# One pool of five PSUM banks, held-back stores, and part of the q norms off TensorE

## The chip, the cores and the metric

The kernel runs on one core of a Trainium2 chip. Its time is the device time in microseconds (us) of one execution; a kernel's figure is the median of several runs. The profile is of one execution of its own, and its times are counted from the start of its span.

The engines are named TensorE (PE in the profile, its weight loads PEld), VectorE (DVE), ScalarE (ACT), GpSimd (POOL) and SyncE (SP). Each runs its instructions in the order in which the program lists them, and waits on semaphores for the others.

## The reference

```python
def _attn_ref(q, k, v, tau):            # B, N, C = 4, 6336, 256
    qn = q / (np.linalg.norm(q, axis=1, keepdims=True) + 1e-06)
    kn = k / (np.linalg.norm(k, axis=1, keepdims=True) + 1e-06)
    s = kn.transpose(0, 2, 1) @ qn / tau
    s = s - s.max(-1, keepdims=True)
    a = np.exp(s)
    a /= a.sum(-1, keepdims=True) + 1e-09
    return (v @ a).astype(np.float32)

def _moe_ref(x, w_h, w_t, b_t):         # x: 25344 x 256, the rows of all batches
    H = np.maximum(x @ w_h, 0.0)
    T = 1.0 / (1.0 + np.exp(-(x @ w_t + b_t)))
    return (T * H + (1.0 - T) * x).astype(np.float32)
```

For each of four batches, q and k (6336 rows of 256 channels, f32) give one 256 x 256 attention matrix over channels: products over the rows, divided by the norms of the columns, and a softmax. Each row of v is then multiplied by that matrix, and the result x goes through a highway layer: two more products, a relu, a sigmoid and a mix.

## The kernel before, in words

**Stage 1.** A batch's rows are taken in 50 steps: 48 of 128 rows, in six chunks of eight steps, and two tail steps of 96 rows. A load of one chunk of q, k or v reads 1 MB of f32 and writes 0.5 MB of f16; it is issued by GpSimd (`load`, L286 and L281). For each step and each half c of the channels, `stage1` makes three matmuls into the PSUM tile `sg[c]`: k by q (256 columns, L393), k by k (128 columns, L394) and q by q (128 columns, L395). The diagonals of the last two are the squared norms of the columns of k and q.

**The chain.** After a batch's last step `plan_chain` makes a softmax out of `sg`: diagonals (VectorE), square roots (GpSimd, `pow`, L452), reciprocals, a broadcast over partitions (TensorE, `cqb`), exponentials (ScalarE), a transposition (`eps`) and a product with the two weight matrices (`fold`, `ah`). It ends in the f16 tile `mr`, which holds the attention matrix and its products with both weights, so that stage 2 needs v alone.

**Stage 2.** The 50 steps of v are taken in 25 pairs a batch; the pairs of all batches are numbered g = 0 to 99. For batches 0 to 2, v is transposed on TensorE (L612) and evicted by VectorE or ScalarE into `vtsb`. For the last batch (`by_dma`) SP issues one DMA transpose a chunk (`transpose_chunk`, L620) into `vT`, of which there are four buffers. Each pair then has three products of four matmuls each, all of line L642: `h`, `t` and `x` (the latter is written into the bank of `d`). ScalarE or VectorE copies the bias into t's bank ahead of t (`bias`, L405 and L407), or in the last part, on odd pairs beyond g = 65, a matmul does (L673). ScalarE makes relu(h)/2 into `d` (L682) and a tanh of t (`gate`, L696); VectorE makes the product (L703) and the result (L722). Results gather in an `o` tile of one chunk (four pairs, 1 MB), which SP stores (L736).

**PSUM.** Of eight banks, `sg0` and `sg1` hold stage 1, `vt` serves the transposes, and five are given by name: `h` two, `d` two, `t` one. After stage 1 of the last batch `sg0` also serves h and `sg1` also serves t.

**What sets the order.** The program is written by a planner. `plan.add` makes a task of one engine with a key (mostly the pair's number g plus an offset: the smallest key of those that can start goes first), a pitch, a latency, the tasks that it depends on, and the buffers that it takes and gives back. `Plan.run` plays this with the planner's own costs and lists the instructions in the order in which they start. Loads go to GpSimd in one fixed order, eight in flight at most; stores and DMA transposes go to SP, by key. On the chip every engine keeps the order so found. `slot_of` spreads the steps of stage 1 of batches 1 to 3 over the pairs: `ENDS = [18, 42, 66]` are the pairs at which the three end. Stage 1 of batch b + 1 so runs among the pairs of batch b.

## Time and profile before

| | |
|---|---|
| median of 7 runs | 279.61 us (279.0 to 280.04) |
| the profiled execution's own time | 278.93 us |
| its span | 277.2 us |
| busy in the span: PE, DVE, ACT, POOL | 254.6, 181.6, 175.1, 54.6 us |
| granted TensorE clock | 0.994 |
| bytes read from and written to HBM | 78.38 MB, 25.95 MB |
| stage 1 of batches 0 to 3 ends at | 38.7, 94.3, 155.4, 216.7 us |
| first matmul of h of pairs 0, 24, 48, 66, 75, 99 | 47.2, 111.2, 172.6, 215.8, 235.7, 269.8 us |
| matmuls of q by q (L395), steps of 128 rows | 384 |
| last load issued, last load landed | 219.8, 234.4 us |

In the profile a line such as `L395 PE MATMUL sg<-q` names the line of the kernel, the engine, the operation and the tiles (written<-read). "Releaser" is what ended an engine's idle time. A line of waits has who waited, for whom, the total in us, how often, and the longest. A line of stretches has the bounds in us, the length, then busy us (and instructions) of PE, PEld, DVE, ACT and POOL, the granted clock, the mean busy share of the 16 DMA engines (above 1 where transfers overlap on an engine) and the GB/s that they moved, counted as written. A line of the list of instructions has start and duration in us. Matmuls are pipelined: a matmul's duration is longer than the distance to the next.

### The profile page before, as it was taken

The page shows a single profiled execution, that of the slowest core. Times are in us where ns is not written, and L with a number is a line of the kernel's source. Part 1 is how long each engine was busy: PE and PEld are TensorE (multiplying, and loading weights), DVE is VectorE, ACT ScalarE, POOL GpSimd, SP SyncE. Part 2 cuts the span into 40 slices and gives each one's busy share as a digit, 9 for nine tenths or more (in the row PEclk, how much of TensorE's full clock was granted, in tenths as well). Part 3 has the DMA queues.
Part 4 walks back from the last instruction along what each step waited for, and adds up shares of the span by engine and source line. Part 5 has one row for each costly group of instructions (what it writes and reads, how often), then busy time and mean ns, then how long its engine had stood idle before and what let it go on. Part 6 is the DMA issues. An engine that isn't in the chain of part 4 may idle for free.

```text
span 277.2 us, 6499 instructions
## 1 busy us (share of the span) xinstructions
PE 254.6 (92%) x2610; PEld 227.7 (82%) x2610; DVE 181.6 (66%) x366; ACT 175.1 (63%) x328; POOL 54.6 (20%) x104
## 2 busy tenths in 40 slices
PE   0797879999999999999999999999999888999992
PEld 0596877899999888999999888999999767888881
DVE  1000035667766886777776886777777887898994
ACT  1000016667767776776767766777767779898982
POOL 7222445220212230211112421111111300000000
PEclk9997999999999999999999999999999999999999
DMA  6999999999999999999999999999999999999984
GB/s 109 212 216 212 208 208 213 215 212 286 263 248 277 285 217 283 245 268 287 237 262 288 254 245 279 222 295 263 248 280 286 233 266 176 356 205 313 269 307 180
DMA packets 29581, 68.80 MB, mean 248 GB/s; under 512 B 14832, under 2 KB 16496, under 8 KB 26608
## 3 DMA queue, kind: packets, MB, share of 16 engines
q0 software_dynamic: 12608, 39.20, 71.5%
q1 hardware_dynamic: 16944, 29.20, 31.5%
q8 instruction: 20, 0.33, 0.4%
q14 instruction: 9, 0.07, 0.1%
HBM read 78.38 MB, written 25.95 MB: 376 GB/s over the span
## 4 chain that ended last, share of the span: by engine, by line
PE 55%; DMA 39%; POOL 2%; DVE 2%; issue 1%; ACT 0%; POOLq 0%; DVEq 0%; ACTq 0%
DMA v<-in_v_dram 19%; PE h L642 11%; PE t L642 11%; PE d L642 10%; PE sg L393 9%; DMA k<-in_k_dram 7%; DMA vT<-v 7%; DMA q<-in_q_dram 7%; PE sg L394 4%; PE sg L395 4%; PE vtps L612 3%; PE t L673 1%; DVE pp L703 1%; POOL q L286 1%; PE ah L551 1%
## 5 line engine op out<-in xcount | busy, mean ns | idle before, releaser
L393 PE MATMUL sg<-q,k 128*128 128x256 f16 x384 | 95.8, 280 | 13.6 <-DMA k<-in_k_dram 13.6
L642 PEld LDWEIGHTS <-vtsb 128*128 128x128 f16 (+1 forms) x900 | 83.4, 99 | 9.8 <-issue 1.9
L394 PE MATMUL sg<-k 128*128 128x128 f16 x384 | 86.2, 225 | 0.0
L395 PE MATMUL sg<-q 128*128 128x128 f16 x384 | 85.4, 222 | 0.0
L703 DVE SCALAR_TENSOR_TENSOR pp<-uu,d 128x512 f32<-128x512 f32 (+1 forms) x100 | 68.4, 685 | 17.2 <-PE d L642 12.0
L696 ACT ACTIVATE uu<-t 128x512 f32<-128x512 f32 (+1 forms) x100 | 59.6, 598 | 27.3 <-PE t L642 25.4
L682 ACT ACTIVATE d<-h 128x512 f32<-128x512 f32 (+1 forms) x100 | 58.4, 584 | 22.3 <-PE h L642 22.0
L722 DVE SCALAR_TENSOR_TENSOR o<-h,pp 128x512 f32<-128x512 f32 x96 | 66.2, 690 | 2.9
L393 PEld LDWEIGHTS <-k 128*128 128x128 f16 x384 | 38.4, 100 | 16.3 <-DMA k<-in_k_dram 14.6
L405 ACT COPY t<-bias_all 128x512 f32<-128x512 f32 (+1 forms) x78 | 46.0, 589 | 2.0
L642 PE MATMUL d<-mr,vtsb 128*128 128x256 f16 x300 | 44.8, 272 | 0.1
L642 PE MATMUL t<-mr,vtsb 128*128 128x256 f16 x300 | 44.8, 272 | 0.1
L642 PE MATMUL h<-mr,vtsb 128*128 128x256 f16 x300 | 44.8, 272 | 0.0
L407 DVE COPY vtsb<-vtps 128x256 f32<-128x256 f32 (+1 forms) x62 | 26.1, 421 | 26.2 <-PE vtps L612 25.9
L395 PEld LDWEIGHTS <-q 128*128 128x128 f16 x384 | 38.6, 100 | 5.4
L394 PEld LDWEIGHTS <-k 128*128 128x128 f16 x384 | 38.6, 100 | 1.9
L642 PEld LDWEIGHTS <-vT 128*128 128x128 f16 x288 | 28.1, 98 | 5.7 <-DMA vT<-v 1.0
L612 PE MATMUL vtps<-ident,v 128*128 128x128 f32 x144 | 27.7, 274 | 1.8 <-ACT vtsb L405 1.1
L441 DVE SCALAR_TENSOR_TENSOR junk<-sg,ident 128x128 f32<-128x128 f32 x16 | 4.6, 287 | 37.0 <-PE sg L395 36.4
L484 ACT COPY gs<-sg 128x256 f32<-128x256 f32 x8 | 2.6, 377 | 37.8 <-DVE junk L441 37.8
L286 POOL DMA_DIRECT2D v<-in_v_dram x24 | 13.1, 544 | 47.0 <-PE d L642 15.5
L286 POOL DMA_DIRECT2D k<-in_k_dram x25 | 13.5, 539 | 42.3 <-DMA k<-in_k_dram 15.7
(66 smaller groups left out, 176.9 us busy)
## 6 DMA issues: line engine op xcount, KB each, us to landing
out_dram<-o SPq DMA_DIRECT2D x23, 1024.0 KB, 8.9
v<-in_v_dram POOLq DMA_DIRECT2D x24, 512.0 KB, 20.6
q<-in_q_dram POOLq DMA_DIRECT2D x23, 512.0 KB, 21.5
k<-in_k_dram POOLq DMA_DIRECT2D x23, 512.0 KB, 20.6
out_dram<-o SPq DMA_DIRECT2D x2, 512.0 KB, 2.6
out_dram<-ot SPq DMA_DIRECT2D x4, 192.0 KB, 6.7
q<-in_q_dram POOLq DMA_DIRECT2D x2, 256.0 KB, 14.5
k<-in_k_dram POOLq DMA_DIRECT2D x2, 256.0 KB, 11.1
```

What stands on the lines that cost most here:

```text
L286: nc.gpsimd.dma_start(out=t[:, s : s + n, :], in_=main_rows(src)[:, j * CH + s : j * CH + s + n, :])
L393: nc.tensor.matmul(sg[c][:, 0:C], kc, qa, start=first, stop=False)
L394: nc.tensor.matmul(sg[c][:, C : C + P], kc, kc, start=False, stop=False)
L395: nc.tensor.matmul(sg[c][:, C + P : C + 2 * P], qa[:, cs], qa[:, cs], start=False, stop=last)
L405: nc.scalar.copy(out=out, in_=in_)
L407: nc.vector.tensor_copy(out=out, in_=in_)
L612: nc.tensor.transpose(ps[:, u, 0:nr], words, ident0[0:nr, 0:nr])
L642: nc.tensor.matmul(out[0:nr, u, :], vt[u][kt][:, 0:nr], mr[kt][:, col * C : (col + 1) * C], **flags(u, kt))
L682: nc.scalar.activation(out=d[0:nr, :, :], in_=ps_t["h", b, i][0:nr, :, :], func=Act.Relu, scale=0.5)
L696: nc.scalar.activation(out=uu[0:nr, :, :], in_=ps_t.pop(("t", b, i))[0:nr, :, :], func=Act.Tanh, scale=-0.5)
L703: nc.vector.scalar_tensor_tensor(out=pp[0:nr, :, :], in0=el.pop(("uu", b, i))[0:nr, :, :], scalar=1.0, in1=ps_t.pop(("d", b, i))[0:nr, :, ...
L722: nc.vector.scalar_tensor_tensor(out=ot, in0=ps_t.pop(("h", b, i))[0:nr, :, :], scalar=0.0, in1=el.pop(("pp", b, i))[0:nr, :, :], op0=AluO ...
```

## The change

- `plan_squares`, `squares`, `sum_squares`: for the first four chunks (`APART = 4`) of batches 1 to 3 the q-by-q matmuls are left out. ScalarE squares the chunk in two halves of 128 x 1024 into f32, GpSimd adds these up to 128 x 256 (three or four additions a chunk, with the one to the batch's sum), two matmuls of one column each sum over the partitions, and VectorE adds the result to the diagonals.
- `Plan.banks`: the five banks that were h, t and d are common. A task that needs one names how many must be free (`spare`: h 3, t and its bias 2, relu and chain steps 1) and takes the one free for longest. `adds` and `sets` note in which banks a matmul may accumulate onto what another engine wrote; `spread` prepares all five (before: three). In the last part `sg0`, `sg1` and `vt` join. The chain takes its banks here too.
- `plan_holds`, `hold`: up to pair 64 (`UNTIL`) the store of a chunk comes after a 1 KB copy on SP that reads the first result of the chunk five later (`LAG`); `o` has seven buffers (before: three). Later stores have keys of at least 65.6.
- Batch 3's chunk 0 of v is transposed on TensorE as f16 (`BY_DMA = 1`); the others by DMA with a key 18 pairs ahead (before: 8); `vT` has three buffers.
- Batch 0's last chunk comes after the tail, in four parts (before: ahead of the tail in the loop, in two parts), and `consts.serial` puts the constants behind the first two loads on GpSimd.
- Buffers: q and k five each (before: nine), v five (before: seven), `vtsb` nine (before: five). Keys come from a table `PRIO` with one offset up to pair 66 and one beyond; `ENDS` is 22.5, 38 and 66; the bias is put in by matmul on even pairs beyond 66; the four matmuls of a product go kt by kt.

```diff
--- before.py
+++ after.py
-QK_BUFS = 9
-V_BUFS = 7
-AHEAD = 8
-MOVE = 100e3
-LOOK = 1.6
-POW = 1.0
-HEAD = 8
-TAIL = 65
+QK_BUFS = 5
+V_BUFS = 5
+O_BUFS = 7
+LAG = 5
+UNTIL = 64
+AHEAD = 18
+BY_DMA = 1
+MOVE = 150e3
+APART = 4
+V_AHEAD = 4
+PRIO = {
+    "tr": (-3.46, 4.45), "ev": (5.77, -0.35), "h": (-3.36, 2.13), "bias": (2.76, -0.39),
+    "t": (-0.61, -1.32), "relu": (0.66, 0.05), "x": (-0.27, -1.65), "gate": (1.05, 1.05),
+    "prod": (-3.53, 1.79), "res": (0.54, -1.85), "s1": (0.08, -2.66), "sq": (3.14, 1.81),
+}
+POW = 0.75
+HEAD = 10
+TAIL = 66
+EVERY = 2
 EV = BIAS = ("ACT", "DVE")
-ENDS = [18, 42, 66]
+ENDS = [22.5, 38, 66]
...
+                and (not x.spare or bank_for(x) is not None)
...
+        def bank_for(x):
+            open_ = [(a, n) for n, (a, _) in self.banks.items() if a is not None and a <= t + eps]
+            if len(open_) < x.spare:
+                return None
+            if x.adds:
+                open_ = [(a, n) for a, n in open_ if self.banks[n][1]]
+            else:
+                open_ = [(a, n) for a, n in open_ if not self.banks[n][1]] or open_
+            return min(open_)[1] if open_ else None
...
         "q": QK_BUFS, "k": QK_BUFS, "v": V_BUFS, "tail_q": 2, "tail_k": 2, "tail_v": 2,
-        "vT": 4, "vT_t": 1, "o": 3, "ot": 1, "uu": 3, "pp": 3, "vtsb": 5, "mr0": 2, "mr1": 2,
-        "sg0": 1, "sg1": 1, "vt": 1, "t": 1, "h": 2, "d": 2,
+        "sq": 2, "vT": 3, "vT_t": 1, "o": O_BUFS, "ot": 1, "uu": 3, "pp": 3, "vtsb": 9, "mr0": 2, "mr1": 2,
+        "sg0": 1, "sg1": 1, "vt": 1,
     }
     for tag, bufs in nbuf.items():
         plan.ring(tag, bufs)
-    pool_of = {tag: psum for tag in ("sg0", "sg1", "vt", "t", "h", "d")}
+    common = [f"c{n}" for n in range(5)]
+    nbuf |= {tag: 1 for tag in common}
+    pool_of = {tag: psum for tag in ["sg0", "sg1", "vt"] + common}
...
     plan_load("q", 0, 0)
     plan_load("k", 0, 0)
     consts = plan.add("POOL", len(plan.tasks), 0.6, 1.5, [], constants)
+    consts.serial = True
     for j in range(1, NJ - 1):
         plan_load("q", 0, j)
         plan_load("k", 0, j)
     for nm in "qk":
         plan_load(nm, 0, NJ)
-    plan_load("q", 0, NJ - 1, 2)
-    plan_load("k", 0, NJ - 1, 2)
+    for part in range(4):
+        plan_load("q", 0, NJ - 1, 4, part)
+        plan_load("k", 0, NJ - 1, 4, part)
...
-                seq.append((NP * b + CH // 2 * j - (10 if b == B - 1 else 2), 1, "v", b, j))
+                seq.append((NP * b + CH // 2 * j - V_AHEAD, 1, "v", b, j))
...
-            nc.tensor.matmul(
-                sg[c][:, C + P : C + 2 * P], qa[:, cs], qa[:, cs], start=False, stop=last
-            )
+            if not apart(b, s // CH):
+                nc.tensor.matmul(
+                    sg[c][:, C + P : C + 2 * P], qa[:, cs], qa[:, cs], start=False, stop=last
+                )
...
+    def apart(b, j):
+        return b > 0 and j < APART
+    sq_t = {}
+    sums = {}
+    def squares(b, j, half):
+        sq_t[b, j, half] = sq = new("sq", [P, CH // 2, C], f32, f"sq{b}_{j}_{half}")
+        qa = tiles[("q", b, j)][:, half * CH // 2 : (half + 1) * CH // 2, :]
+        nc.scalar.activation(out=sq, in_=qa, func=Act.Square)
+    def sum_squares(b, j, step):
+        add = partial(nc.gpsimd.tensor_tensor, op=AluOp.add)
+        if step == 0:
+            sq, other = sq_t[b, j, 0], sq_t.pop((b, j, 1))
+            add(out=sq, in0=sq, in1=other)
+        elif step == 1:
+            sq = sq_t[b, j, 0]
+            add(out=sq[:, 0:2, :], in0=sq[:, 0:2, :], in1=sq[:, 2:4, :])
+        else:
+            sq = sq_t.pop((b, j, 0))
+            if j == 0:
+                sums[b] = small.tile([P, C], f32, tag="sums", name=f"sums{b}")
+                add(out=sums[b], in0=sq[:, 0, :], in1=sq[:, 1, :])
+            else:
+                add(out=sq[:, 0, :], in0=sq[:, 0, :], in1=sq[:, 1, :])
+                add(out=sums[b], in0=sums[b], in1=sq[:, 0, :])
...
+    def plan_squares(b):
+        ends, x = {}, None
+        for j in range(APART):
+            key = slot_of((b - 1) * NS + CH * j) + PRIO["sq"][0]
+            parts = [
+                plan.add(
+                    "ACT", key, 0.97, 1.07, loaded("q", b, CH * j + CH // 2 * n),
+                    lambda j=j, n=n: squares(b, j, n), take=["sq"],
+                )
+                for n in range(2)
+            ]
+            ends[j] = parts
+            n0 = len(plan.tasks)
+            y = plan.add(
+                "POOL", key, 2.36, 2.45, parts, lambda j=j: sum_squares(b, j, 0), drop=[(parts[1], "sq")]
+            )
+            y = plan.add("POOL", key, 1.27, 1.35, [y], lambda j=j: sum_squares(b, j, 1))
+            x = plan.add(
+                "POOL", key, 1.3 if j else 0.65, 1.4 if j else 0.75, [y] + ([x] if x else []),
+                lambda j=j: sum_squares(b, j, 2), drop=[(parts[0], "sq")],
+            )
+            for z in plan.tasks[n0:]:
+                z.soft = True
+        def over_partitions():
+            sums[b, "ps"] = ps = new("vt", [P, 2], f32, f"sumps{b}")
+            for c in range(2):
+                nc.tensor.matmul(
+                    ps[:, c : c + 1], sums[b][:, bass.ts(c, P)], ones[:, 0:1], start=c == 0, stop=c == 1
+                )
+        def keep():
+            sums[b, "sb"] = sb = small.tile([P, 2], f32, tag="sumsb", name=f"sumsb{b}")
+            nc.vector.tensor_copy(out=sb, in_=sums[b, "ps"])
+        p = plan.add("PE", key + 2, 0.4, 0.6, [x], over_partitions, take=["vt"])
+        return ends, plan.add("DVE", key + 1, 0.15, 0.22, [p], keep, drop=[(p, "vt")])
...
+        def rest_of_q():
+            if sums_of_q:
+                xq = st["x"][:, 0:2]
+                nc.vector.tensor_tensor(out=xq, in0=xq, in1=sums[b, "sb"], op=AluOp.add)
+        dq = dve(
+            lambda: (diagonal(0), diagonal(1), rest_of_q()), 0.9, 0.95, [last, consts] + sums_of_q
+        )
         nq = pool(lambda: norm(0), POW, POW + 0.2, [dq])
         dk = dve(lambda: (diagonal(2), diagonal(3)), 0.75, 0.8, [dq])
...
+        if b == B - 1:
+            gs.joins = [("sg0", True), ("sg1", True)]
...
-            st["cqb"] = new("vt", [P, C], f32, f"cqb{b}")
+            st["cqb"] = new(cqb.bank, [P, C], f32, f"cqb{b}")
...
-        cqb = pe(bcast, 0.43, [iq], take=["vt"])
+        cqb = pe(bcast, 0.43, [iq])
+        cqb.spare, cqb.sets = 1, False
...
+                tr0.spare, tr0.sets = 1, False
...
-            fo = pe(lambda c=c: fold(c), 0.43, [et[c]] + w_ld, take=["h"])
+            fo = pe(lambda c=c: fold(c), 0.43, [et[c]] + w_ld)
+            fo.spare, fo.sets = 1, True
...
+            if natural(b):
+                for kt in range(2):
+                    nc.tensor.transpose(
+                        ps[:, u, :].bitcast(f16)[:, kt * P : kt * P + nr],
+                        v[:, bass.ts(kt, P)],
+                        ident[0:nr, 0:nr],
+                    )
+            else:
+                nc.tensor.transpose(ps[:, u, 0:nr], v.bitcast(f32), ident0[0:nr, 0:nr])
 
...
+        for kt, u in ((0, 0), (0, 1), (1, 0), (1, 1)):
+            nc.tensor.matmul(
+                ps_t[kind, b, i][0:nr, u, :],
+                vt[u][kt][:, 0:nr],
+                mr[kt][:, col * C : (col + 1) * C],
+                start=fresh and kt == u == 0,
+                stop=kt == u == 1,
+                skip_group_check=True,
+            )
+    def bank(kind, b, i):
+        ps_t[kind, b, i] = x = new(bank_of[kind, b, i].bank, [P, 2, C], f32, f"{kind}{b}_{i}")
+        return x
...
+    def by_matmul(b, i):
+        g = b * NP + i
+        return g > TAIL and g % EVERY == 0
...
+    def spread(n):
+        ps_t[n] = new(spreads[n].bank, [P, 2, C], f32, f"bias_{n}")
+        nc.tensor.matmul(ps_t[n], row0, btb, start=True, stop=True)
...
+    plan.banks = {tag: [0.0, False] for tag in common}
+    spreads = []
+    for n in range(len(common)):
+        sp = plan.add("PE", -1, 0.22, 0.5, b_ld + [consts], lambda n=n: spread(n))
+        sp.spare, sp.sets = 1, True
+        spreads.append(sp)
+    b_all = plan.add("ACT", 0.5, 0.5, 0.63, spreads, spread_out, drop=[(sp, "bank") for sp in spreads])
+    begun, chunk_stores = {}, []
+    def hold(b, j):
+        nc.sync.dma_start(out=held_row, in_=og[(b, j)][0:1, 0, :])
+    def plan_holds():
+        for x, b, j in chunk_stores:
+            n = b * NJ + j + LAG
+            y, g = begun.get(n, (None, 1e9))
+            if g > UNTIL:
+                x.key = max(x.key, UNTIL + 1.6)
+                continue
+            x.key = g + 1.6
+            plan.add(
+                "SP", g + 1.5, 0.1, 0, [y], lambda n=n: hold(n // NJ, n % NJ), size=1024,
+            )
...
+        part_ends, sums_of_q = ({}, []) if not apart(b, 0) else plan_squares(b)
+        for n, s in enumerate(order_of(b)):
+            key = -100 + n if b == 0 else slot_of((b - 1) * NS + s) + PRIO["s1"][0]
...
+                "PE", key, 0.33 if apart(b, s // CH) else 0.44, 0.66, deps, lambda s=s: stage1(b, s),
+                take=["sg0", "sg1"] if n == 0 else [],
+                drop=([] if apart(b, s // CH) else drops("q", b, s)) + drops("k", b, s),
+            )
+            x.lat = x.pitch if n < NS - 1 else 0.66
+            if apart(b, s // CH) and s % CH == CH - 1:
+                plan.add("NONE", 0, 0, 0, [x] + part_ends[s // CH], None, drop=drops("q", b, s))
...
+            h = bank_of["h", b, i] = plan.add(
+                "PE", pr("h", g), 0.435, 0.64, [ev] + ready[b], lambda i=i: main_h(b, i)
+            )
+            h.spare, h.sets = 3, True if rows(2 * i) == P else None
...
+            own.spare = 2
+            h_before[:] = [h]
+            r = bank_of["d", b, i] = plan.add(
+                "ACT", pr("relu", g), 0.5, 0.63, [h, own], lambda i=i: relu(b, i)
+            )
+            r.spare, r.adds = 1, True
...
+                begun[b * NJ + j] = (y, g)
...
-                plan.add(
+                z = plan.add(
                     "SP", g + 2, 0.1, 0, [y], lambda j=j, o=o, n=n: store(b, j, o + 2 - n, n),
                     drop=[(own_o, "o")] if o + 2 == CH else [], size=P * n * C * 4,
                 )
+                chunk_stores.append((z, b, j))
...
+    plan_holds()
+    plan.add("NONE", 0, 0, 0, uses_vt, None).joins = [("vt", False)]
...
```

## The prediction

> **What bounds the kernel now.** First the head of the page (busy time, the slices with the DMA rows, the HBM total):
>
> ```profile
> span 277.2 us, 6499 instructions
> PE 254.6 (92%) x2610; PEld 227.7 (82%) x2610; DVE 181.6 (66%) x366; ACT 175.1 (63%) x328; POOL 54.6 (20%) x104
> ...
> DMA  6999999999999999999999999999999999999984
> ...
> HBM read 78.38 MB, written 25.95 MB: 376 GB/s over the span
> ```
>
> then the table of stretches:
>
> ```profile
> 22.00:39.00 17.00, 14.07 (x164) 12.54 (x161) 0.29 (x2) 0.00 (x0) 5.69 (x10) 0.90 1.09 211
> 51.00:65.00 14.00, 14.00 (x154) 12.97 (x153) 9.17 (x16) 9.75 (x17) 2.65 (x5) 1.00 1.06 229
> 110.00:155.00 45.00, 45.00 (x486) 41.71 (x485) 33.60 (x57) 32.56 (x56) 7.95 (x15) 1.00 1.06 261
> 155.00:211.00 56.00, 55.42 (x592) 50.68 (x591) 42.10 (x89) 40.79 (x76) 10.96 (x20) 1.00 1.06 262
> 235.00:265.00 30.00, 29.35 (x258) 25.27 (x259) 27.20 (x42) 26.83 (x52) 0.00 (x0) 1.00 1.06 282
> 265.00:277.00 12.00, 6.95 (x61) 5.87 (x59) 8.29 (x13) 6.29 (x13) 0.00 (x0) 1.00 0.64 257
> ```
>
> TensorE idles 0.6 us between 51 and 211 us, and the DMA engines are never free until 265 (share 1.01 and more). GB/s counts bytes as written, and loads halve (f32 to f16): the loads-only stretch at 211 moves 422 GB/s of reads; 261 in the mixed one is 318 read (159 written) plus 102 stored, 420 together. So DMA too runs flat out: 104.3 MB at 0.42 MB/us is 248 us, and with 4.9 us before the first bytes and about 4 idle at the end, some 20 us are left for seven transposes. Two resources are full at once, and I look at who waits:
>
> ```profile
> PE sg L393 <- DMA k<-in_k_dram: 13.6, 5, 9.0
> POOL k L286 <- DMA v<-in_v_dram: 15.4, 8, 3.6
> SPq L620 <- DMA v<-in_v_dram: 12.8, 1, 12.8
> ```
>
> TensorE waits for k only at the start, and loads wait for the eighth before them. Landing against first use, chunk by chunk: batch 3's k land at 155, 165, 175, 184, 196, 205 us and are read at 159, 167, 177, 187, 196, 206. Data come just in time, so relief of TensorE counts only as far as loads come earlier too.
>
> **The skill.** Its "DMA: Bandwidth & Descriptors" (Where 436 GB/s comes from) puts the ceiling at 435 GB/s; the trace's 422 agrees, so the rate has no reserve. "SBUF — State Buffer" (Who interferes with whom) says that VectorE with at most one SBUF input, outside its two-port modes, doesn't contend with GpSimd; product and result read one operand from PSUM. No run here shows it.
>
> **Part 1: q norms off TensorE.** 32 of 50 steps of batches 1 to 3 lose both q·q matmuls: 192. The price is the distance of starts in the list of instructions:
>
> ```profile
> 15.11 0.22 PE L395 MATMUL sg<-q 128*128 128x128 f16 x1
> 15.17 0.27 PE L393 MATMUL sg<-q,k 128*128 128x256 f16 x1
> 15.28 0.22 PE L394 MATMUL sg<-k 128*128 128x128 f16 x1
> 15.33 0.22 PE L395 MATMUL sg<-q 128*128 128x128 f16 x1
> ```
>
> L395 to L393 is 0.055 us (its 222 ns overlap the next): 192 x 0.055 = 10.6 us less, in stretches where TensorE has no idle. Added: 24 ACT squares of 128x1024. By the skill's "ScalarE: Activation LUTs" (What ACT_TABLE_LOAD costs: 186 ns + 0.833 ns an element) 1.04 us each; the same gives 0.61 at 512, where the trace has 0.58 to 0.60. 25 us in some 160, on an ACT 72% busy (40.8 of 56); by the build's order VectorE (75%) takes over 30 bias copies and gives ACT 28 evictions of vT: both end at 80 to 85%, hidden by TensorE, and at most 25 us if not. The first two squares stand on ACT ahead of the copy of batch 0's sums and wait for batch 1's first q, 2 us after the last k (37.9 against 35.9); behind them waits only the scaling, and its other arm (diagonals, pow, broadcast) takes about 4 us from the last step as well: 0, at most 2. GpSimd: 2048 elements of adds a chunk; the skill's "GPSIMD Engine Reference" (Performance versus the Vector engine) has 4497 ns for 2048, so 12 x about 5 us = 60 us (40 to 90). The trace has no such add. Loads stand behind them in POOL's queue, but eight loads are in flight (20.6 us to landing), so 5 us of delay starves nothing. The sums end in two tiny TensorE matmuls a batch, 0.2 us each: 0.6. If POOL is late, TensorE, in order, stands: the build's order puts batch 1's directly behind POOL's last add, 1 to 2 us.
>
> **Part 2: banks.** Five banks go to whoever is next, where h had two, d two, t one. A pair's banks are held about 8 us in sum (matmuls 0.44, each eviction 0.6 to 0.7): 1.6 us a pair from five, 1.0 to 1.2 in the tail from seven or eight, below the pace of 2.4 and 1.4 us. Value 0; end costs -2 (the tail loses some stalls) to +3.
>
> **Part 3: start.** The first load is issued ahead of the identity, so 0.65 us earlier (1.42 against 0.74 for the identity's memset). The last q and k chunks come in quarters, tail ahead: 2 steps of 0.43 remain after the last landing and not 6: 1.7. The quarters come in 1 KB packets, 97 ns each in the trace's DMA records against 325 for 4 KB: 63 ns more for each of 256 rows of 4 KB is 1.0 us over 16 engines, of which the halves of today (173 ns for 2 KB, 21 more a row) cost 0.3: about 0.7. Net -1.7.
>
> **Part 4: held stores.** A chunk's store waits until five more chunks are begun, by a 1 KB copy ahead of it on SP; until pair 64 that takes about six stores, 6.3 MB or 15 us at 0.42, out of the loads' way. No byte vanishes: they return after pair 64. When the last k of batch 3 is in: now 71.7 MB read and 15.9 stored at 0.42 is 208, plus 4.9 = 213 (landed 214.2). Then: the build's order has one v chunk fewer ahead of it, 70.6 read + 9.8 stored = 191.4, + 4.3 + 0.7 + 1 = 197.4. TensorE alone: batch 3's sums end at 216.7, less 10.6, less 1.7, and the order now has six pairs fewer ahead (six of 1.53 = 9.2): 195.8 with the 0.6. The load is 1.6 us late: I take 1.5 (0 to 4). The eleven 1 KB copies hold up SP alone, behind which only stores stand (in the last ones' case the first transposes too, whose v isn't in before). Buffers for q and k go from 9 to 5, v from 7 to 5: a load that finds none stops POOL's queue. Eight in flight are about three of each, which leaves two being read, and DMA needs just one or two in flight to stay busy: 0, at most 3.
>
> **Part 5: the end.** Chunk 0 of batch 3 is transposed by TensorE: 16 x 0.055 = 0.9 us (1.8 if as dear as f32) and four evictions, shared by ACT and VectorE; DMA loses one transpose, about 3 us. Bias matmuls 17 to 16, two more bank seeds: +0.2. From pair 75 on TensorE sets the pace:
>
> ```profile
> L642 PE MATMUL h<-mr,vT x96: 269/273/283, 235.7 to 268.8; 128*128 128x256 f16 x96
> ```
>
> 96 matmuls are 24 pairs, 1.41 us each. SP's queue then: six stores come free at once near pair 65, 15 us, with 3.4 MB of v loads (8) and vT of chunk 3 (3) ahead of its use at pair 87, some 30 us later; vT of chunk 4 waits for the third vT buffer, freed at pair 82, nine pairs (13 us) before its use; behind it stand two stores and the next vT. DMA has about 44 us of work against 48 of TensorE: hidden, with 4 us of cover.
>
> Sum on the profiled execution: 277.2 - 10.6 - 1.7 + 0.6 + 1.1 + 1.5 = 268.1. Its own time is 278.93, 1.7 above its span, and the median of the runs 0.7 above that: 268.1 + 2.4 = 270.5 us, 3.3% less.
>
> **Rivals.**
> A, TensorE and DMA mesh poorly: with two full resources and an order fixed at build time, each late load stops both, and half the relief is lost; or the bytes decide: 277.2 - 0.6 (start) - 3 (one transpose) + 0.7 = 274.3, median 276.7. For it: DMA share above 1 to 265 us. Against: stores alone move 459 GB/s (249 to 251 us) against 420 in the mix, and the last 12 us have room (0.64). 274 to 278: 0.19.
> B, slower: POOL becomes the bound. If adds cost 10 us a chunk (twice the skill's figure), POOL needs 120 + some 40 of issue and chain in about 160 us; loads then run dry, k comes late by what is over, and beyond 10.5 us of lateness the kernel loses. At 11 us a chunk, 12 us late: 282. For it: adds and loads share one queue in order. Against: POOL is 20% busy, and the eight in flight. 0.08.
> C, the held stores and flexible banks also remove the stalls around the last softmax chain (TensorE 21.6 of 24 us at 211 to 235): -4, 266.5, below 267: 0.13.
> D, squares and POOL cost what TensorE gained, within 0.2%: 0.02.
> The forecast, 267 to 274: 0.58.
>
> The range: A to D and the forecast together from 265.0 to 278.0; what lies outside is B, D and a small part of C. The likeliest case's own is 267 to 274. A difference within 0.2% (0.56 us) can't be told from none. Faster 0.90, same 0.02, slower 0.08.
>
> **What would show it.** L395 x192 and a TensorE some 9 us less busy; squares near 1.04 us; POOL near 110 us busy; stores landing late until pair 64, then bunched; batch 3's sums ending near 198 and pair 66 near 207. Wrong if TensorE waits for k by more than 4 us after 51 us, for POOL's sums by over 2 us, for vT in the tail, or if ACT's evictions fall behind.

## The result, and the profile after

The changed kernel takes 286.29 us in the median of 12 runs (275.01 to 291.57) where the kernel before takes 279.35 (278.87 to 280.12, 31 runs): 2.5% slower by the medians, where 270.5 was forecast. The run-to-run spread is a result in itself: 6% against 0.5%. (The comparison of fast runs, 0.987 with an interval of 0.9845 to 0.9895, takes only the two runs within 1.5% of the kernel's fastest; the profiled run, of 283.15 us, isn't one of them.)

The page of the changed kernel, its head:

```profile
span 281.4 us, 6279 instructions
PE 248.4 (88%) x2447; PEld 219.9 (78%) x2447; DVE 185.8 (66%) x375; ACT 182.5 (65%) x354; POOL 115.6 (41%) x153
...
PEclk9999998999999999999999999999999999799995
...
GB/s 114 214 214 209 206 208 213 214 214 213 214 209 214 214 215 284 227 285 276 227 280 275 225 285 266 241 291 245 256 247 148 150 127 341 410 279 261 328 426 242
...
HBM read 78.38 MB, written 25.95 MB: 371 GB/s over the span
```

TensorE is relieved, by 6.2 us of busy time (254.6 to 248.4) where some 9 were forecast, and the bytes are the same. New are slices 31 to 33 of the 40 (211 to 232 us), some 150 GB/s in a kernel that moves 206 to 291 in the slices ahead of them (the first apart), and a clock that drops behind them. Its groups of instructions, on part 1 of the prediction:

```profile
L480 ACT ACTIVATE sq<-q 128x1024 f32<-128x1024 f16 x24 | 24.7, 1051 | 36.2 <-DMA q<-in_q_dram 36.2
...
L465 PE MATMUL sg<-q 128*128 128x128 f16 x192 | 42.8, 223 | 0.0
...
L486 POOL TENSOR_TENSOR sq<-sq,sq 128x1024 f32<-128x1024 f32 x12 | 28.4, 2364 | 11.7 <-ACT sq L480 11.7
```

The sizes of part 1 came as forecast: 192 matmuls left, squares of 1051 ns, and adds of 2364 + 1283 + 738 + 729 ns, 5.1 us a chunk. Its table of stretches:

```profile
155.00:211.00 56.00, 54.41 (x546) 48.87 (x544) 45.21 (x96) 42.83 (x86) 24.04 (x28) 1.00 1.09 257
211.00:222.00 11.00, 10.86 (x98) 9.25 (x96) 9.92 (x17) 10.52 (x24) 1.57 (x3) 1.00 1.09 161
222.00:235.00 13.00, 12.66 (x118) 11.05 (x117) 9.09 (x14) 11.26 (x22) 0.00 (x0) 1.00 1.20 161
235.00:250.00 15.00, 9.96 (x76) 7.98 (x76) 10.09 (x16) 8.67 (x17) 0.00 (x0) 0.89 1.08 358
250.00:265.00 15.00, 15.00 (x135) 12.97 (x133) 14.11 (x22) 13.70 (x27) 0.00 (x0) 1.00 1.09 287
265.00:281.00 16.00, 6.44 (x56) 5.35 (x53) 8.28 (x13) 5.71 (x12) 0.00 (x0) 0.77 0.88 347
```

The same two stretches from 211 us on in the kernel before:

```profile
211.00:222.00 11.00, 9.87 (x100) 8.72 (x98) 9.29 (x28) 7.93 (x18) 3.01 (x5) 1.00 1.06 268
222.00:235.00 13.00, 11.71 (x96) 9.30 (x93) 10.54 (x22) 11.10 (x25) 0.00 (x0) 1.00 1.12 206
```

In the changed kernel DMA stays as busy by its share between 211 and 235 us (1.09, 1.20), but moves 161 GB/s. Then TensorE works 9.96 of 15 us, and from 265 on, where it is nearly done, DMA still has a share of 0.88. Who waits, after 211 us:

```profile
POOL v L341 <- DMA vT<-v: 12.7, 1, 12.7
...
DVE o L890 <- DMA out_dram<-o: 6.4, 1, 6.4
PE d L819 <- ACT d L853: 6.0, 2, 5.4
ACT d L853 <- DVE o L890: 5.5, 1, 5.5
```

and the chain of waits at that place:

```profile
212.37 9.62 SPq L783
...
222.04 16.49 DMA out_dram<-o
238.62 0.70 DVE o L890
239.41 0.59 ACT d L853
240.04 1.01 PE d L819 x4
```

Read upwards: TensorE's product x (tile `d`) waits for ScalarE's d, that for VectorE's result (of chunk 18, counted from 0 over all batches), and that for a free one of the seven `o` buffers, which the held store of chunk 11 gives back. SP issued that store at 222.04, after the DMA transpose that kept its queue from 212.37 on (9.62 us), and it landed at 238.5. How long its transposes took from issue to landing, as the view of the tile vT of the changed kernel has it:

```profile
DMA to landing us min/median/max: 7.1/14.1/26.3
```

and the same view of the kernel before:

```profile
DMA to landing us min/median/max: 5.5/7.0/18.1
```

The median doubled. The place where the time went is found by the first h of pair 75 (235.7 us in the kernel before):

```profile
L819 PE MATMUL h<-mr,vT x80: 272/273/417, 240.8 to 268.2; 128*128 128x256 f16 x80
L819 PE MATMUL h<-mr,vtsb x16: 272/272/273, 229.3 to 232.9; 128*128 128x256 f16 x16
```

Pair 75 begins at 229.3, 6.4 us sooner; from there to the end of the span it takes 52.1 us against 41.5, 10.6 more: 277.2 - 6.4 + 10.6 = 281.4. The forecast had -10.2 (-10.6 - 1.7 + 0.6 + 1.5) and +1.1. So there are two errors in this execution, 3.8 us ahead of pair 75 and 9.5 behind it.

### The profile page after: what moved, and what is told of

Read it like the earlier page. It is cut to its first block, busy times and chain, and to the rows that moved or that the text cites. A ratio compares the mean times of both kernels' runs of the same rounds, so it can differ in the third digit from the quotient of the medians.

```text
span 281.4 us, 6279 instructions
## 1 busy us (share of the span) xinstructions
PE 248.4 (88%) x2447; PEld 219.9 (78%) x2447; DVE 185.8 (66%) x375; ACT 182.5 (65%) x354; POOL 115.6 (41%) x153
## 4 chain that ended last, share of the span: by engine, by line
PE 63%; DMA 19%; SPq 4%; DVE 4%; POOL 3%; ACT 3%; issue 2%; ACTq 0%; DVEq 0%; POOLq 0%
DMA k<-in_k_dram 13%; PE d L819 12%; PE t L819 12%; PE sg L462 11%; PE h L819 11%; DMA out_dram<-o 6%; PE sg L463 6%; PE vtps L775 5%; SPq L783 3%; PE sg L465 2%; ACT d L853 1%; DVE pp L871 1%; POOL sq L486 1%; PE cqb L640 1%; PE t L848 1%
## 5 line engine op out<-in xcount | busy, mean ns | idle before, releaser
L819 PEld LDWEIGHTS <-vtsb 128*128 128x128 f16 (+1 forms) x948 | 90.2, 99 | 19.1 <-issue 9.0
L462 PE MATMUL sg<-q,k 128*128 128x256 f16 x384 | 86.5, 280 | 15.4 <-DMA k<-in_k_dram 15.3
L463 PE MATMUL sg<-k 128*128 128x128 f16 x384 | 79.5, 225 | 0.0
L819 PE MATMUL d<-mr,vtsb 128*128 128x256 f16 x316 | 47.6, 274 | 6.6 <-ACT d L853 5.9
L480 ACT ACTIVATE sq<-q 128x1024 f32<-128x1024 f16 x24 | 24.7, 1051 | 36.2 <-DMA q<-in_q_dram 36.2
L465 PE MATMUL sg<-q 128*128 128x128 f16 x192 | 42.8, 223 | 0.0
L486 POOL TENSOR_TENSOR sq<-sq,sq 128x1024 f32<-128x1024 f32 x12 | 28.4, 2364 | 11.7 <-ACT sq L480 11.7
L543 ACT COPY t<-bias_all 128x512 f32<-128x512 f32 (+1 forms) x49 | 28.8, 592 | 0.0
L819 PEld LDWEIGHTS <-vT 128*128 128x128 f16 x240 | 23.9, 100 | 4.4 <-issue 0.3
L341 POOL DMA_DIRECT2D v<-in_v_dram x24 | 13.3, 555 | 31.4 <-DMA vT<-v 12.7
L545 DVE COPY t<-bias_all 128x512 f32<-128x512 f32 (+1 forms) x35 | 23.9, 683 | 0.0
L341 POOL DMA_DIRECT2D q<-in_q_dram x27 | 15.0, 556 | 20.5 <-DMA q<-in_q_dram 7.7
```

Of the source, the lines that this page charges most:

```text
L341: nc.gpsimd.dma_start(out=t[:, s : s + n, :], in_=main_rows(src)[:, j * CH + s : j * CH + s + n, :])
L462: nc.tensor.matmul(sg[c][:, 0:C], kc, qa, start=first, stop=False)
L463: nc.tensor.matmul(sg[c][:, C : C + P], kc, kc, start=False, stop=False)
L465: nc.tensor.matmul(sg[c][:, C + P : C + 2 * P], qa[:, cs], qa[:, cs], start=False, stop=last)
L486: add(out=sq, in0=sq, in1=other)
L543: nc.scalar.copy(out=out, in_=in_)
```

## The experiments

Each time is a median, and each ratio is to the kernel before, run beside it on the same chip (its medians there were 279.1 to 279.3 us).

**Which part does it.** Three theories stood against each other. Theory 1: DMA transposes that run beside loads hold the DMA engines up. Theory 2: the held stores alone do. Theory 3: the squares and adds give part 1's gain back.

e1 is the changed kernel with its DMA transposes due 8 pairs ahead again:

```diff
-AHEAD = 18
+AHEAD = 8
```

> One number is changed against the changed kernel: a transpose by DMA is due 8 pairs ahead of its use, as in the kernel before, and not 18. The five held stores of chunks 11 to 15 then stand ahead of every transpose on SP, and no transpose meets a load of batch 3's v before about 225 us. Theory 1 (transposes that run beside loads hold the DMA engines up, the held stores wait behind them, and the ring of seven result buffers stops VectorE): the five stores land about 2.5 us apart from 214 on, no result waits for a buffer, TensorE works 14.5 of the 15 us at 235 to 250, and the median falls from 286 to 272-277 with a spread under 2%. Theory 2 (the bunch of held stores alone fills the engines, with or without transposes): chunk 18's result still waits over 4 us, median 282-290, spread 4% and more. Theory 3 (the gain was lost in the steady part, to squares and adds): the tail is about as before, 275-279, and TensorE's stretches ahead of 211 us don't move.

289.53 us (288.90 to 291.28), slower still. The stores landed from 216 to 239 us and no result waited for a buffer, so theory 2 fails; but the 272 to 277 us of theory 1 failed as well. vT of chunk 1, issued at 224.3, landed at 251.4 together with v of chunk 5 (issued 229.9, landed 249.9), and TensorE worked 0.15 of the 15 us from 235 to 250. The transposes met the loads later, not less.

e2 is the changed kernel without held stores:

```diff
-UNTIL = 64
+UNTIL = -1
...
             if g > UNTIL:
-                x.key = max(x.key, UNTIL + 1.6)
+                pass
```

> The changed kernel without the held stores (no 1 KB copies, each store due as soon as its chunk is done), transposes still due 18 pairs ahead. Theory 1: vT of chunks 1 and 2 still land 14 to 20 us after their issue, but with few stores behind them the ring of seven holds, so the stall at 232-238 us is gone or under 2 us: median 274-280, spread under 2%. Theory 2: transposes land in 5 to 8 us, median 272-276. Also: if holding stores back was what brought batch 3's k early, k is now read with under 1 us to spare or late, and batch 3's sums end at 203-206 us rather than 201.6; if not, within 1 us of 201.6.

283.53 us (283.31 to 285.31): lower than the changed kernel's median, within its spread, and steady. vT of chunks 1 to 3 took 4.9, 12.3 and 11.0 us to land, the last two beside loads. Without holding, k is read with 0 to 5 us to spare, and batch 3's sums end at 213.3 us instead of 201.6: holding stores back is worth 11.7 us at that place (roughly, as e2's plan has another order), and was paid back in the tail.

e3 makes q by q on TensorE in every step; the tasks for squares, adds and sums stay in the plan, and so in its order, but do nothing:

```diff
-            if not apart(b, s // CH):
+            if True:
...
-                    lambda j=j, n=n: squares(b, j, n), take=["sq"],
+                    None, take=["sq"],
```

> The changed kernel in its own order, with all q norms back on TensorE (192 matmuls more) and without the squares on ScalarE, the adds on GpSimd and the sums over partitions. My step for part 1 (10.6 us of TensorE in stretches without idle, less 0.6): batch 3's sums end 8 to 11 us later than 201.6, at 210-212, and pair 66 starts at 221-224. Theory 3 (squares and adds give back what TensorE gained): they end at 200-205, within 3 us. For the end: theory 1 puts the stall after 211 us into DMA, which this doesn't touch, so the time is 285-295, at most as much above the changed kernel as the sums are later.

287.72 us (287.21 to 289.71). Batch 3's sums end at 211.5 and pair 66 starts at 222.9 (201.6 and 213.0 in the changed kernel), 9.9 us later. Pair 0 already begins 2.3 us later in this profile (51.1 against 48.8, after twice as long a time at half clock), so 7.6 to 9.9 us are part 1's, of the 10.0 that were forecast. Theory 3 fails. The median is only 1.4 us above that of the changed kernel, which fits a tail set by DMA.

e4 is the kernel before with its transposes due 18 pairs ahead:

```diff
-AHEAD = 8
+AHEAD = 18
```

> The kernel before with one number of the change: its transposes due 18 pairs ahead and not 8 (four vT buffers, stores not held, three result buffers). Theory 1: vT of chunks 0 to 3 run beside v's loads and the last k's, land 10 to 20 us after issue, stores behind them stop the three result buffers: 283-292 us and a spread of 2% and more, where the kernel before has 0.5%. Theory 2 (only held stores matter): 278-281 and a spread under 1%.

290.39 us (286.27 to 294.42): one number of the change makes the old kernel 3 to 4% slower (1.0307, 1.0236 to 1.0378) and unsteady, with a spread of 2.8%. vT of chunk 2 took 20.9 us beside v of chunks 4 and 5.

**The disputed cost by itself.** e5 and e9 compute nothing of the reference; they only move data, stage by stage. This is the third stage of e5, with its constants put in and comments added:

```python
    gate(V, V + Bt)             # waits for the stage before, frees the targets of this one
    for n in range(6):
        load(b[n], 1, n)        # GpSimd's queue, f32 to f16
        if n < 4:
            transpose(n)        # SP's queue
```

> No kernel of this computation: it leaves all of the reference's arithmetic out and only moves data, stage after stage, each begun when the one before has landed: (1) six loads of 1 MB (f32 to f16, from GpSimd's queue), (2) four transposes of 0.5 MB of f16 from SP's queue, (3) six loads and four transposes at once, (4) four stores of 1 MB, (5) four stores and four transposes in turn on SP, (6) six loads and four stores, (7) six loads, four stores and four transposes, (8) four plain f32 loads from ScalarE's queue beside four transposes. Theory 1 (a transpose and a casting load in flight together hold each other up): (1) takes about 15 + 2 us and (2) 12 to 20 us, but (3) takes 40 us or more, well over their sum, and (7) as much over (4), (1) and (2) added up; (5) and (6) are about the sum of their parts. Theory 2 (only the amount of bytes counts): every mixed stage takes the sum of its parts within 15%.

| stage of e5 | us, first issue to last landing | sum of the parts |
|---|---|---|
| 6 loads | 17.5 | |
| 4 transposes | 11.9 | |
| 6 loads, 4 transposes | 35.8 | 29.4 |
| 4 stores | 11.4 | |
| 6 loads, 4 stores | 27.6 | 28.9 |
| 6 loads, 4 stores, 4 transposes | 37.6 | 40.8 |
| 4 stores and 4 transposes in turn, one queue (from the end of the stage before) | 21.8 | 23.3 |
| 4 plain loads, 4 transposes | 21.8 | loads not measured alone |

The result lies between the two theories: one mixed stage lost 6.4 us, the others none. But where a second queue was at work, the first transpose came late: 17, 22 and 15 us from issue to landing, 4.4 alone. The DMA queues of e5 from 147 to 159 us, in the stage with all three (q0 are the casting loads, q1 is SP's):

```profile
DMA packets 1282, 2.53 MB, mean 211 GB/s; under 512 B 705, under 2 KB 705, under 8 KB 1282
...
q0 software_dynamic: 641, 2.36, 97.1%
q1 hardware_dynamic: 641, 0.16, 9.9%
```

and from 42 to 57 us, in the stage of loads and transposes:

```profile
DMA packets 1844, 1.98 MB, mean 132 GB/s; under 512 B 1447, under 2 KB 1447, under 8 KB 1844
...
q0 software_dynamic: 436, 1.63, 85.7%
q1 hardware_dynamic: 1408, 0.35, 27.0%
```

In the former, 641 packets of the loads (577 of 4 KB and 64 of 4 B) stand against 641 of 256 B. That is how the Trainium skill's "DMA: Bandwidth & Descriptors" (Queues, rings and completion order) has it: an engine goes round its queues packet by packet. The loads lose 8% (2.36 MB in 12 us is 197 GB/s as written, 213 alone), while a transpose moves 0.16 MB in 12 us and starves, and with it all that stands behind it on SP. In the latter little gets on: 132 GB/s, and 20 of the 397 load packets of 4 KB in the DMA records took 2 to 5 us (all took 0.32 in the former).

e9 asks whether the order decides. It has two transposes in each stage, and three loads or stores beside them:

> Data movement alone again; all of the reference's arithmetic is left out. Three turns of two stages: three casting loads begun 1.8 us ahead of two transposes, then two transposes begun 1.8 us ahead of three casting loads. After them two turns of: two transposes 1.8 us ahead of three plain f32 loads from ScalarE's queue, and two transposes 1.8 us ahead of three stores from ScalarE's queue. Theory 1 as it stands now (a casting load that is issued while a transpose is in flight makes both collapse; a transpose issued behind loads merely waits for them): loads first takes 14 to 16 us each turn, all packets under 1 us; transposes first takes 20 to 30 us, with load packets of 2 us and more. If the kind of load matters, the stages with ScalarE's queue take 14 to 18 us without such packets; if any transfer does it, they take 20 to 30 too. Rival: order doesn't matter, both orders within 2 us of each other.

Loads first: 14.2, 14.3, 14.1 us. Transposes first: 15.3, 15.4, 15.4, with no packet over 1.4 us. The order isn't what makes them collapse, so theory 1 in that form fell. Plain loads from ScalarE's queue: 14.5 and 14.3. Stores from ScalarE's queue: 21.1 and 21.0 us, with 12 packets of 2 to 5.4 us each time. So the collapse is real and was seen only with a transpose and a second queue at work, but what sets it off stays open.

**Keeping them apart.** e6 transposes four of batch 3's chunks on TensorE and begins the tail's pairs in order:

```diff
-BY_DMA = 1
+BY_DMA = 4
...
-                "PE", pr("h", g), 0.435, 0.64, [ev] + ready[b], lambda i=i: main_h(b, i)
+                "PE", pr("h", g), 0.435, 0.64, [ev] + ready[b], lambda i=i: main_h(b, i), follows=h_before[:] if g > TAIL else []
```

> The changed kernel with four of batch 3's six full chunks transposed by TensorE (one in the changed kernel), so that DMA transposes just chunks 4, 5 and the tail, after nearly all loads are in; in the tail pairs also begin in order. Cost on TensorE 24 x 0.11 us and on ACT or VectorE twelve evictions of 0.6 us. Theory 1: the held stores land from 212 us on 2.5 us apart, nothing waits for a result buffer or for vT before pair 91, and TensorE sets the end: 270-274 us with a spread under 1.5%. Theory 2 (held stores alone stop VectorE): a wait of 4 us and more for a result buffer stays, 278-288.

283.34 us (282.97 to 284.41): theory 1's 270 to 274 missed. The stores did land in time, but v of chunk 5 wasn't issued before 229.6, 2 us behind vT of chunk 4; they landed at 247.7 and 250.6, and DMA moved 79 GB/s from 235 to 250. The load had waited 13.0 us for a buffer of v to come free. That pointed to `V_BUFS`, which none of these runs had touched.

e7, on top of e1:

```diff
-V_BUFS = 5
+V_BUFS = 7
```

> The kernel of e1 (transposes due 8 pairs ahead) with seven buffers for v as in the kernel before, and not five, so that the last loads of v don't wait for a transpose to free a buffer: all are in by about 226 us. Theory 1: no load beside the transposes any more; vT of chunk 1 still stands behind six stores and lands near 240 us, 5 to 8 us after pair 79 could start, the others 2 to 5 us after they are issued; 276-281 us where e1 has 289.5. If the stores in front are what makes transposes slow, it stays at 287-290.

277.67 us (274.61 to 279.28), 12 us less than e1 by two buffers. The last loads were issued at 206.5 to 207.1 and in by 222.6, vT of chunk 1 landed at 239.0 behind seven stores, and TensorE stood 3.4 us for it. Time and landings are as expected; the wait was put at 5 to 8 us.

e10 is e7 with the `follows` of e6 and

```diff
-BY_DMA = 1
+BY_DMA = 2
```

> The kernel of e7 (seven v buffers, transposes due 8 pairs ahead) with two chunks of batch 3 transposed by TensorE and not one, pairs of the tail begun in order. All loads are issued before the first transpose, and vT of chunk 2, due at pair 83 near 238 us, stands behind seven stores and lands at 237-241. Theory 1: no collapse of the DMA engines, the 6 us stall of e7 shrinks to 0-3 us, with it the half clock after it: 270-274 us. Rival (the tail is bound by bytes on DMA whatever the order): 276-279 as e7.

274.83 us (274.23 to 276.13; 0.9837 of before, 0.9801 to 0.9874), just above theory 1's 270 to 274. No engine waits for a transpose by DMA or for a result buffer after 200 us.

**The buffers alone.** e12 is the changed kernel with one constant of the kernel before:

```diff
-V_BUFS = 5
+V_BUFS = 7
```

> The changed kernel with seven buffers for v and nothing else: transposes still due 18 pairs ahead, so vT of chunk 1 is issued at 204 us and v of the last chunk and the tail at 206-208, behind it. Theory 1: those two loads and vT of chunk 1 still collapse (landing 8 to 14 us later than in e7's 220 us for the load), and the held stores wait behind: 278-287 us with a spread over 1%, faster than the changed kernel's 286 because one collapse remains and not two. If seven buffers were the whole cure, it is 272-277 like e7 or below.

275.09 us (274.98 to 275.19; 0.984, 0.9816 to 0.9865): 11.2 us and the whole spread of 6% gone by one constant; the rival, the buffers as the whole cure, is right, and theory 1's 278 to 287 wrong. Two of the changed kernel's twelve runs, of 275.01 and 276.60 us, come as low, so its delay doesn't strike every time; no such run was profiled. Up to pair 66 it runs like the changed kernel (214.2 us against 213.0). Its stretches after that:

```profile
211.00:222.00 11.00, 10.73 (x95) 9.15 (x95) 9.92 (x20) 10.53 (x25) 0.00 (x0) 1.00 1.18 202
222.00:235.00 13.00, 13.00 (x123) 11.41 (x121) 11.75 (x19) 12.39 (x25) 0.00 (x0) 1.00 1.04 391
235.00:250.00 15.00, 15.00 (x135) 12.97 (x133) 14.09 (x22) 13.71 (x27) 0.00 (x0) 1.00 1.14 284
250.00:265.00 15.00, 15.00 (x133) 12.95 (x132) 14.12 (x22) 13.55 (x27) 0.00 (x0) 1.00 1.04 355
```

One stretch of 202 GB/s remains at 211 to 222, where vT of chunk 1 (204.9 to 221.2) still meets v of chunk 5; then DMA moves 391 and TensorE has no idle up to 265. v of chunk 4 was issued at 196.8 where the changed kernel issued it at 218.96. There it had to wait for a buffer until vT of chunk 1 had landed, at 218.4 (the 12.7 us of POOL above); v of chunk 5 and the tail stood behind it, and all three met vT of chunk 2.

e13, in the kernel before, and e14, in the changed one:

```diff
-V_BUFS = 7
+V_BUFS = 5
...
-V_BUFS = 5
+V_BUFS = 6
```

> The kernel before with five buffers for v instead of seven, nothing else: transposes due 8 pairs ahead, stores not held, four vT buffers. If the buffers tie v's last loads to the transposes here too, v of the last chunks is issued after the first two transposes, they meet in flight, and vT of chunks 1 and 2 come late for pairs 79 and 83: 282-292 us. If it needs the held stores or the early due times to do harm: 279-281.

> The changed kernel with six v buffers. One load of a whole chunk and the tail's then still wait for a transpose to free a buffer, where five leave two or three and seven none or one: if buffers are the cause, between the two, 276-283 us, with a spread over 1%; as fast as with seven (275) if six are enough.

e13 takes 290.25 us (289.21 to 293.51; 1.0431), e14 282.58 (279.12 to 287.50). Five, six, seven buffers give 286.3, 282.6, 275.1 in the changed kernel, and in the old one five cost 11 us, with nothing held back. Both results lie where they were expected if the buffers are the cause. Who waits in e13, from 200 us on:

```profile
POOL v L286 <- DMA vT<-v: 16.8, 1, 16.8
...
PEld L642 <- DMA vT<-v: 8.8, 3, 6.5
...
PE h L642 <- DMA vT<-v: 8.0, 3, 6.2
```

The first of these waits tells the slow kernels from the others. From 185 us on, loads of v wait for a DMA transpose to give a buffer back in the changed kernel (12.7 us), e2 (16.7), e3 (5.6), e4 (21.8), e8 (17.3), e13 (16.8) and e14 (17.7), and 13 us at a time for transposes of batch 3 on TensorE in e1 and e6: in all that take 282 us and more. In the kernel before and in the six at 273 to 278 us no load waits for a DMA transpose, and none over 4.7 us at a time for TensorE's. e4 has seven buffers and waits all the same, since its transposes are due 18 pairs ahead. So too few buffers is one way into this wait and not the only one.

**The 3.8 us ahead of pair 75.** e8 is the changed kernel with the old start:

```diff
-        return [*range(S - CH), *range(S, NS), *range(S - CH, S)]
+        return list(range(NS))
...
-    for part in range(4):
-        plan_load("q", 0, NJ - 1, 4, part)
-        plan_load("k", 0, NJ - 1, 4, part)
+    plan_load("q", 0, NJ - 1, 2)
+    plan_load("k", 0, NJ - 1, 2)
```

> The changed kernel with batch 0's last q and k chunk loaded in halves ahead of no other step, as in the kernel before (the tail's steps last again). My step for part 3 says the new start is worth 1.7 us, so pair 0 begins at 50.5 where the changed kernel has 48.8. Against it: batch 1's first k (40.4 us in both kernels) sets the pace, TensorE only idles longer ahead of it (2.96 us against 1.54) and then runs at half clock until 45 us: then, with the old start, no half clock at 41 to 45, and pair 0 begins at 46.5-47.5. The end has the tail's stall as before: 283-290 us.

Pair 0 begins at 47.7 us (48.8 in the changed kernel), 1.1 sooner and not 1.7 later. Batch 1's first k, on which TensorE waits next, lands at 40.5 to 40.7 in both. The list of TensorE's instructions of the changed kernel, the first with its idle time before it:

```profile
40.74 0.28 PE L462 MATMUL sg<-q,k 128*128 128x256 f16 x1 [2.96 <-DMA k<-in_k_dram]
...
41.57 0.41 PE L462 MATMUL sg<-q,k 128*128 128x256 f16 x1
```

(in the kernel before 1.54 us idle, and 0.27 us for such a matmul after it). The stretches of the changed kernel:

```profile
41.00:43.00 2.00, 2.00 (x15) 1.56 (x13) 0.79 (x3) 0.67 (x3) 1.57 (x4) 0.64 1.07 209
43.00:45.00 2.00, 2.00 (x15) 1.61 (x13) 1.21 (x6) 0.42 (x2) 1.22 (x3) 0.50 1.08 217
```

of e8:

```profile
43.00:45.00 2.00, 1.68 (x18) 1.32 (x16) 1.25 (x6) 1.01 (x5) 1.32 (x3) 1.00 1.07 215
```

and of e15, which is told below:

```profile
43.00:45.00 2.00, 2.00 (x26) 1.86 (x25) 1.53 (x8) 1.47 (x5) 1.94 (x4) 1.00 1.09 219
```

After 2.96 us of idle the clock (third figure from the end) is 0.5, after the 1.54 of the kernel before and the 1.77 of e8 it stays at 1. The Trainium skill's "TensorE: Matmul & The Clock Gate" (What's actually happening) has it fall to half after an idle window of about 3.4 us; these traces agree on the length but not on the idleness: in e4 1.72 us of idle were enough. Rather, the clock follows windows that are less than about half busy. In all 16 traces that have a clock record, the clock changes only after whole multiples of 3.41 us. Cut into such windows, the traces show this: all 37 drops to half came behind a window with 1.70 us of matmuls or less (0.83 here in the changed kernel, 1.70 in e4), and the 1158 windows behind which the clock stayed full had 1.46 us or more (1.73 here in e8). Half clock ended behind windows with 2.80 us or more and went on behind those with up to 2.46. The time of e8, 290.57 us (285.41 to 293.18), says only that the tail was as bad.

e11 is e10 with that old start. e15 and e16 are e12 and e10 with 34 matmuls in the idle time, right after batch 0's last step, into a bank that nobody reads (the task that runs them is left out here):

```diff
+    def warm():
+        ps = new("vt", [P, 2, P], f32, "warm")
+        for n in range(34):
+            nc.tensor.matmul(ps[:, n % 2, :], row0, ident, start=True, stop=True)
...
```

> The kernel of e10 with the start of the kernel before (last q and k chunk of batch 0 in halves, tail's steps last). If the start's new order costs 1.1 us through the half clock, as e8's pair 0 said (47.7 against 48.8), this is 0.5 to 1.5 us faster than e10, and pair 0 begins at 47-48; if my step was right it is 1.7 us slower.

> The kernel of e12 (seven v buffers) with 34 matmuls into a bank that nobody reads, after batch 0's last step, in the idle time of about 3 us before batch 1's first k; it computes what e12 does, 1.9 us of TensorE's work added. If the half clock at 41 to 47 us comes from that idle time and costs what it seems to: no half clock there, pair 0 begins at 46.0-47.5 where e12 has 50.4, and the time is 1.5 to 3.5 us under e12's 275.1, 271.5-273.6. If not, pair 0 begins as late as before or later, and the time is 275-277.

> The kernel of e10 (loads before all transposes, two chunks by TensorE) with the same 34 matmuls: pair 0 at 46.0-47.5 where e10 has 48.8, and 1 to 2 us under e10's 274.8: 272.5-274 us. If the half clock isn't the cause: 274.5-276.

e11 takes 277.18 us, 2.4 more than e10, against both forecasts: pair 0 began at 47.6, but the new plan lost TensorE 2.5 us and the clock after it at 95 to 110, in batch 1's chain. e15 takes 273.65 (273.49 to 275.16; 0.981, 0.9779 to 0.984), the lowest of all and just above its 271.5 to 273.6, with pair 0 at 48.1 (50.4 in e12; the first k came 1 us later in this profile than in most); the intervals of the two overlap. e16 takes 274.82, as e10, and misses its 272.5 to 274: pair 0 is 1.6 us sooner (47.2), pair 12 no longer (78.8 against 78.7), because TensorE waits 1.0 us for k of batch 1's fifth chunk, which lands at 75 us. So the idle time is shown as the cause of the half clock, whose price is 0 to 1.4 us: until 75 us the loads set the pace.

## Why the prediction was wrong, step by step

- **Part 4, the buffers: the step that failed, at a price of 0 to 3 us.** "Buffers for q and k go from 9 to 5, v from 7 to 5 ... DMA needs just one or two in flight to stay busy: 0, at most 3." It asked whether DMA would idle, and DMA never did. What a missing buffer does is move the last loads to after the first transposes: v of chunk 4 went out at 218.96 us and not at 196.8. It cost 11.2 us (e12), with 282.6 at six buffers between, and 11 us in the old kernel (e13).
- **Part 5, SP's queue: "hidden, with 4 us of cover".** It took transposes at 3 us in a row. Beside other transfers they took 14.1 us in the median from issue to landing (7.0 in the kernel before, whose first one took 18.1 too: that line was in the trace). The held stores stood behind them. With seven buffers the tail from pair 75 took 42.9 us (230.4 to 273.3), and the forecast of 42.6 (41.5 + 1.1) holds.
- **Part 3, the start: -1.7.** Measured +1.6 at pair 0 (48.8 against 47.2), 3.3 of the 3.8 us. The step counted TensorE's work after the last landing, not the next load that it waits for, though "data come just in time" was my own reading, and I applied it to part 4 alone.
- **Part 4, the held stores: +1.5 (0 to 4).** The idea held, the 1.5 did not come: after 51 us k was never late in the changed kernel, and holding is worth 11.7 us at batch 3's end (e2).
- **Part 1: -10.6 + 0.6.** Right in kind and about in size: 7.6 to 9.9 (e3); POOL 115.6 us against 110, and TensorE waited 0.4 us for its sums. From pair 0 to pair 75 the changed kernel takes 8.0 us less than the one before (180.5 against 188.5), where parts 1 and 4 together had 8.5.
- **Part 2: 0.** No wait for a bank shows apart from those behind the result buffers; not tested alone.
- **Rivals.** A's number, 274 to 278, is where the kernel with seven buffers lies, but its reason isn't: k came up to 13 us early. Its 459 GB/s for stores alone is not a rate that lasts: in e5 four stores of 1 MB landed 2.49 us apart, 421 GB/s. B failed (5.1 us a chunk, not 11). A transfer that comes late had no slower rival of its own, so slower got 0.08.

## What to carry over

Price a stream's buffer count by when the last loads are issued and what is in flight then, not only by whether the engine idles. Keep DMA transposes away from loads still to be issued, and let nothing urgent stand behind one on its queue. Move work into a stage only after pricing what that stage's own limit is. A spread that grew from 0.5% to 6% was the sign of such a meeting here, and went with it (e12: 0.1%, in four runs).

## What the runs showed of the hardware

A transpose of 0.5 MB lands 4.4 us after its issue alone and 15 to 22 us beside four to six loads (e5), where one 256 B packet of it goes with one packet of the loads. At times both nearly stop: 25 GB/s from 224 to 228 us in the changed kernel, at a DMA share of 1.25, with 0.33 us for a 256 B packet in the median where it takes 0.018 alone. Three casting loads beside two transposes never did so in six turns, three stores from ScalarE's queue did in two of two; the trigger wasn't found.

TensorE's clock was halved for the next 3.41 us, or longer, behind windows of that length in which its matmuls filled less than about half (at most 1.70 us), and not by idle time of one certain length.
